# Low parts of queries and keys on GpSimd, a later place in ScalarE's queue for a gated tile's split, and a ninth tile for the first pairs' outputs

## The chip, the cores and the metric

The kernel runs on one core of a Trainium2 chip. The metric is the device time of one execution in microseconds (us), as the median of several timed runs. The engines are named as in the profile: PE is TensorE, DVE is VectorE, ACT is ScalarE, POOL is GpSimd, SP is SyncE, which issues all the transfers (DMAs) here.

## What is computed

Three stages follow each other, all in float32 as far as the reference goes:

```python
scores = q @ k.T / sqrt(64) - log(448)          # 4 batches x 12 heads, 448 x 64
x = sigmoid(scores) @ v                          # back to 1792 tokens x 768
xn = x / sqrt(mean(x * x) + 1e-6) * rms_g
g = xn @ w_gate                                  # 768 -> 1536
h = g * sigmoid(g) * (xn @ w_val)
x2 = h @ w_out                                   # 1536 -> 768
out = ((x2 @ w1) * (x2 @ w2) @ w3) @ w_out2      # 768 -> 1024 -> 1024 -> 768
```

The weights and q, k, v arrive as 64-bit floats.

## The kernel before

**Precision.** TensorE multiplies a rounded form of float32 (`F32R`). An operand that has to be exact is split into two such tiles: a high part (a copy that rounds, by ACT or POOL) and a low part (operand minus high part). `mm3` (L294) then makes three matmuls per block: low weights by high data, high weights by low data, high by high (L296, L297, L298). `split2` (L310) splits an activation: ACT copies at L312 (or POOL at L314), DVE subtracts at L315. `split_weight` (L124) splits a weight: copy on ACT (L126) or POOL (L128), subtraction on POOL (L129). Weights that arrive as 64-bit floats are first turned into float32 by five DVE operations, `to_float` (L106, L107, L108, L116, L119).

**Order.** A scheduler orders each engine's instructions when the program is built, so the written order is a priority and not the order on the engine. Every engine then runs its own queue strictly in order.

**Stages.** A *pair* is two heads, 24 in all. The first 12 pairs (two batches) run at the start: `visit` computes the scores of a pair (`scores`, four column blocks c; L390), ACT takes their sigmoid (L407, L419, L421), `attend` multiplies them with the values (L430, L434), and `take_out` copies the result to a tile `xr` (L457), squares it on ACT (L465, L468) and lets POOL add the squares (L469). These tiles stay on the chip until the normalised x of their batch is made from them (`load_x`, L499, on DVE). There are eight such tiles (`A1`, `xr=8`).

Beside and after these pairs, `w3o_group` multiplies w3 by w_out2 beforehand (L339 to L341; ACT copies the result out, L343). Then `a_group` (L608) makes a gated tile `h` for each of 12 row blocks m and two batches b: a group with `which == 0` gives g, ACT takes its sigmoid (L621) and DVE multiplies (L622); the group with `which == 1` gives the value product, DVE multiplies again (L626) and `split2` splits the tile into `hm` (L312 on ACT, L315 on DVE). In the first six row blocks the groups of b = 1 borrow the PSUM tiles of the attention scores (`psa`).

The other 12 pairs run beside the second half of these groups and beside the first five `b_group` (x2 = h @ w_out; ACT copies out at L635). For these pairs q and k are split too: `load_qk` loads them (L374), and `split_qk` makes the high part on ACT (L381) and the low part on DVE (L382), 128 x 960 elements in one instruction. Their scores (L394) need both parts. The tail of the program (from about 530 us) is further products in a seven-product block scheme (`winograd`).

Of the kernel before, what the change touches and what calls it, by code (L numbers as in the profile page):

```python
# [11 lines left out]
AF = mybir.ActivationFunctionType  # L12
ALU = mybir.AluOpType
# [30 lines left out]
def fused_kernel(ctx: ExitStack, tc: tile.TileContext, qkv, wg, wv, wo, w1, w2, w3, wo2, gam, out):  # L44
    nc = tc.nc

    def pool(name, side=None, space=None):
        kw = {}
        if side:
            kw["side"] = side  # L50
        if space is not None:
            kw["space"] = space
        return tc.alloc_tile_pool(name=name, bufs=1, **kw)
# [29 lines left out]
    def scratch(name):  # L83
        return scr.tile([P, S], F32, tag="s", bufs=6, name=name)
# [215 lines left out]
    def accumulate(tiles, xts, ps=None):  # L300
        ps = psm()[:, :S] if ps is None else ps
        n = len(xts)
        j = 0
        for t, kt in tiles:
            for kw in range(kt):
                mm3(ps, t, kw, xts[j], j == 0, j == n - 1)
                j += 1
        return ps

    def split2(dst, src, scalar=True):  # L310
        if scalar:
            nc.scalar.activation(dst[:, 0, :], src, AF.Copy)  # L312
        else:
            nc.gpsimd.tensor_copy(out=dst[:, 0, :], in_=src)  # L314
        nc.vector.tensor_tensor(out=dst[:, 1, :], in0=src, in1=dst[:, 0, :], op=ALU.subtract)  # L315
# [30 lines left out]

    A1 = dict(raw=3, a=5, al=2, xr=8, wd=2)
    A2 = dict(raw=1, v=2, qk=1, a=3, al=2, xr=2)  # L350
    att = {"bufs": A1, "pool": pool("att1", "left")}

    def at(shape, dtype, tag):
        return att["pool"].tile(shape, dtype, tag=tag, bufs=att["bufs"][tag], name=tag)

    raw, probs, av, acc = {}, {}, {}, {}
# [19 lines left out]
    def split_qk(p):  # L376

        if p < NP:
            t, v, r = at([P, 2, V0], F32R, "qk"), at([P, RAWW - V0], F32, "v"), qk_raw.pop()
            nc.sync.dma_start(out=v, in_=qkv[p // HP, p % HP][:, V0:])  # L380
            nc.scalar.activation(t[:, 0, :], r, AF.Copy)  # L381
            nc.vector.tensor_tensor(out=t[:, 1, :], in0=r, in1=t[:, 0, :], op=ALU.subtract)  # L382
            raw[p] = (t, v)

    def score(ps, p, ds, k):
# [50 lines left out]
    def visit(p, n):  # L436


        if n[0] < p < n[1]:
            scores(p, 3)  # L440
        if p > n[0]:
            attend(p - 1)
            take_out(p - 1)
            if p + n[2] < n[1] and p < NA:
                load_pair(p + n[2])
        if p < n[1]:
            for c in range(3 if p > n[0] else 4):
                scores(p, c)
            if p >= NA:
                split_qk(p + 1)  # L450
                load_qk(p + 2)
# [54 lines left out]
    def split_x(b, k):  # L506

        if k < KD:
            ready.append(load_x(b, k))
        if k:  # L510
            t = acts["x", b, k - 1] = x_tile("x", b)
            split2(t, ready.pop(0), b == 1)
# [7 lines left out]
    def right_blocks(k, b11, b12, b21, b22):  # L520

        tt = nc.vector.tensor_tensor

        def put(j, bl, src):
            t = acts["w", j, k] = right_tile(f"w{j}", bl)
            split2(t, src)

        t1 = scratch("t1")
        put(0, 0, b11)
        tt(out=t1, in0=b12, in1=b11, op=ALU.subtract)  # L530
        put(5, 1, t1)
        put(2, 0, b21)
        tt(out=t1, in0=b22, in1=t1, op=ALU.subtract)
        put(1, 2, t1)
        tt(out=b12, in0=b22, in1=b12, op=ALU.subtract)
        put(3, 2, b12)
        tt(out=b21, in0=b21, in1=t1, op=ALU.subtract)
        put(4, 2, b21)
        put(6, 1, b22)
# [47 lines left out]
    def a_winograd(m):  # L587
        def done(b, g, v):
            s = scratch("s")
            nc.scalar.activation(s, g, AF.Sigmoid)  # L590
            nc.vector.tensor_tensor(out=s, in0=g, in1=s, op=ALU.mult)
            nc.vector.tensor_tensor(out=s, in0=s, in1=v, op=ALU.mult)
            acts["h", b, m] = t = h_tile("hm", m)
            split2(t, s)

        winograd(i_a2, m, done)
# [10 lines left out]
    def h_tile(name, m):  # L607
        return pools[f"h{int(m >= KF1 // 2)}"].tile([P, 2, S], F32R, tag="h", bufs=KF1, name=name)  # L608
# [3 lines left out]
    def a_group(m, b, which):  # L612
        t = W.get(i_a[m][which])
        ps = None
        if b and m < KF1 // 2:

            ps = ps_sc.tile([P, 2, 512], F32, tag="sc", bufs=2, name="psa")[:, 0, :S]
        ps = accumulate([(t, 6)], [acts["x", b, k] for k in range(KD)], ps)
        if which == 0:
            s = scratch("s")  # L620
            nc.scalar.activation(s, ps, AF.Sigmoid)  # L621
            nc.vector.tensor_tensor(out=s, in0=ps, in1=s, op=ALU.mult)  # L622
            half[m, b] = s
        else:
            s = half.pop((m, b))
            nc.vector.tensor_tensor(out=s, in0=ps, in1=s, op=ALU.mult)  # L626
            t = h_tile("hm", m)
            split2(t, s)
            acts["h", b, m] = t

    def b_group(g, m, b):
        t = [(W.get(i), 6) for i in (i_b2 if g else i_b)[m]]
        ps = accumulate(t, [acts["h", b, k] for k in range(KF1)])
        y = scratch("yf")
        nc.scalar.activation(y, ps, AF.Copy)  # L635
        d = yd[g, b, m] = dram.tile([P, S], F32, name=f"y{g}{b}{m}")
        nc.sync.dma_start(out=d, in_=y)
# [8 lines left out]
    def a_units():  # L646
        for m in range(KF1):
            for b in range(2):
                for which in range(2):
                    yield 3.4, (lambda m=m, b=b, w=which: a_group(m, b, w)), i_a[m][which]  # L650

    def b_units(g):
        for m in range(KD):
            for b in range(2):
                yield 6.8, (lambda m=m, b=b: b_group(g, m, b)), (i_b2 if g else i_b)[m][1]
# [62 lines left out]
    a = list(a_units())  # L718
# [7 lines left out]
    pools["h1"] = pool("h1", "right")  # L726
    load_qk(NA)
    split_qk(NA)
    load_qk(NA + 1)
    visits = []  # L730
# [3 lines left out]
    for j, u in enumerate(beside):  # L734
        spent += run(u, int(j >= half_a and j % 2 == 1))

        if 1 <= j <= 3:
            for c in ((0, 1), (2,), (3,))[j - 1]:
                scores(NA, c)
            if j == 3:  # L740
                split_qk(NA + 1)
                load_qk(NA + 2)
            visits = list(range(NA + 1, NP + 1))
        while j > 3 and visits and NP + 1 - NA - len(visits) < (NP + 1 - NA) * (spent - 8.0) / (total - 8.0):
            visit(visits[0], (NA, NP, 1))
            if visits.pop(0) == NA + HP:
                rms_norm(2)
# [93 lines left out]
```

## Time and profile before

| | |
|---|---|
| median of three timed runs | 1113.01 us (1110.99 to 1113.87) |
| the profiled execution, its own time | 1109.31 us |
| its span, first to last instruction | 1107.4 us |
| mean granted TensorE clock | 0.989 |
| busy, share of span: PE, DVE, POOL, ACT | 97%, 73%, 43%, 36% |

A busy PE is not a PE at its peak: a matmul of 448 columns is shown as about 0.37 us long, while the next begins 0.2 us after it. So PE's losses are read from the waits (which engine it waited for, how long), from the windows (how much of a stretch, at which granted clock), and from the chain of waits (the work that ended last, followed back from the end). A group of instructions is named by its line, its engine and its tiles, as in `L382 DVE TENSOR_TENSOR qk<-raw,qk`.

### The profile page before, as it was taken

What the parts mean: (1) busy time and instruction counts of PE and PEld (TensorE: products, weight loads), DVE (VectorE), ACT (ScalarE), POOL (GpSimd) and SP (SyncE); (2) the same over time, 40 slices, a digit from 0 to 9 for tenths busy, and PEclk for the clock granted to TensorE, in tenths of its full rate; (3) what the DMA queues carried; (4) which work ended last, traced back from release to release, by engine and by line L of the source; (5) the groups of instructions that cost most, each with busy time, mean ns of one, the idle gap of its engine ahead of it and who ended that gap; (6) DMA issues with size and microseconds to landing.
All of it is one profiled execution on the core that took longest, in us unless ns stands there. A gap on an engine that the chain in (4) does not pass through costs nothing.

```text
span 1107.4 us, 14309 instructions
## 1 busy us (share of the span) xinstructions
PE 1075.0 (97%) x5236; PEld 907.6 (82%) x5236; DVE 813.4 (73%) x1066; ACT 398.6 (36%) x719; POOL 472.3 (43%) x382
## 2 busy tenths in 40 slices
PE   9989999997899998999999999999999999999998
PEld 4337899995677775799889988999999999999997
DVE  5988998898456688579899989776777645777500
ACT  5764201111444442414544443133443344333221
POOL 2655443443034323333566664222656424656320
PEclk9989999998899999999999999999999999999999
DMA  6733454567445477664212212766221243210131
GB/s 252 253 138 129 148 175 142 166 199 255 138 140 167 130 238 242 200 205 145 82 58 70 73 59 85 235 251 222 84 77 65 67 156 116 91 57 30 48 99 50
DMA packets 62710, 153.25 MB, mean 138 GB/s; under 512 B 6064, under 2 KB 32816, under 8 KB 62640
## 3 DMA queue, kind: packets, MB, share of 16 engines
q1 hardware_dynamic: 62640, 152.33, 40.9%
q8 instruction: 42, 0.69, 0.3%
q14 instruction: 28, 0.23, 0.1%
HBM read 114.95 MB, written 37.36 MB: 138 GB/s over the span
## 4 chain that ended last, share of the span: by engine, by line
PE 64%; DVE 7%; DMA 2%; ACT 2%; issue 1%; POOL 1%; SPq 0%; DVEq 0%; ACTq 0%; POOLq 0%
PE psm L296 10%; PE w L296 10%; PE psm L297 10%; PE w L297 10%; PE psm L298 10%; PE w L298 10%; PE av L434 2%; DVE wf L108 1%; PE psm L394 1%; DVE wf L116 1%; DMA wd<-in_wo 1%; DVE mag L107 1%; PE sc L394 1%; POOL ws L129 1%; DVE wf L119 1%
## 5 line engine op out<-in xcount | busy, mean ns | idle before, releaser
L296 PE MATMUL w<-w,ws 128*128 128x448 f32 x588 | 216.8, 369 | 1.6 <-DVE c L574 1.3
L297 PE MATMUL w<-w,ws 128*128 128x448 f32 x588 | 216.2, 368 | 0.0
L298 PE MATMUL w<-w,ws 128*128 128x448 f32 x588 | 215.6, 367 | 0.0
L129 POOL TENSOR_TENSOR ws<-wf,ws 128x768 fp32r<-128x768 f32 (+1 forms) x88 | 149.5, 1699 | 136.1 <-ACT ws L126 131.9
L129 POOL TENSOR_TENSOR ws<-wd,ws 128x384 fp32r<-128x384 f32 x112 | 126.3, 1142 | 94.9 <-ACT ws L126 86.9
L129 POOL TENSOR_TENSOR ws<-s,ws 128x384 fp32r<-128x384 f32 x84 | 97.2, 1162 | 79.0 <-ACT ws L126 77.3
L128 POOL CAST ws<-wf 128x768 fp32r<-128x768 f32 (+1 forms) x52 | 46.8, 900 | 185.4 <-PE psm L298 90.9
L296 PEld LDWEIGHTS w<-w,ws 128*128 128x128 f32 x588 | 110.3, 188 | 14.6 <-issue 3.7
L298 PEld LDWEIGHTS w<-w,ws 128*128 128x128 f32 x588 | 110.4, 188 | 10.9
L297 PEld LDWEIGHTS w<-w,ws 128*128 128x128 f32 x588 | 110.4, 188 | 10.4
L296 PE MATMUL psm<-hm,ws 128*128 128x448 f32 x288 | 106.7, 370 | 0.0
L297 PE MATMUL psm<-hm,ws 128*128 128x448 f32 x288 | 105.8, 367 | 0.0
L298 PE MATMUL psm<-hm,ws 128*128 128x448 f32 x288 | 105.2, 365 | 0.0
L312 ACT ACTIVATE hm<-s 128x448 fp32r<-128x448 f32 x48 | 27.8, 579 | 213.8 <-DVE s L626 156.8
L108 DVE TENSOR_SCALAR wf<-mag 128x768 uint32<-128x768 uint32 (+1 forms) x76 | 64.4, 847 | 39.4 <-POOL ws L129 35.7
L116 DVE SCALAR_TENSOR_TENSOR wf<-wd,wf 128x768 uint32<-128x768 uint32 (+1 forms) x76 | 86.3, 1136 | 2.3
L296 PE MATMUL psm<-x,ws 128*128 128x448 f32 x216 | 82.0, 380 | 6.1 <-ACT w3ot L343 3.4
L119 DVE SCALAR_TENSOR_TENSOR wf<-wd,wf 128x768 uint32<-128x768 uint32 (+1 forms) x76 | 80.2, 1055 | 1.4
L297 PE MATMUL psm<-x,ws 128*128 128x448 f32 x216 | 80.1, 371 | 0.0
L298 PE MATMUL psm<-x,ws 128*128 128x448 f32 x216 | 79.9, 370 | 0.0
L106 DVE TENSOR_SCALAR mag<-wd 128x768 uint32<-128x768 uint32 (+1 forms) x76 | 49.3, 649 | 32.1 <-DMA wd<-in_wo 21.1
L126 ACT ACTIVATE ws<-wd 128x384 fp32r<-128x384 f32 x112 | 54.6, 514 | 50.2 <-PE w L298 36.3
(131 smaller groups left out, 2159.1 us busy)
## 6 DMA issues: line engine op xcount, KB each, us to landing
wd<-in_wo SPq DMA_DIRECT2D x20, 768.0 KB, 5.7
wd<-in_w SPq DMA_DIRECT2D x16, 768.0 KB, 5.0
wd<-w SPq DMA_DIRECT2D x32, 384.0 KB, 3.4
wd<-in_wg SPq DMA_DIRECT2D x12, 768.0 KB, 4.6
wd<-in_wv SPq DMA_DIRECT2D x12, 768.0 KB, 4.8
wd<-in_w SPq DMA_DIRECT2D x16, 512.0 KB, 4.5
raw<-in_qkv SPq DMA_DIRECT2D x11, 736.0 KB, 4.2
w<-wf SPq DMA_DIRECT2D x16, 384.0 KB, 2.6
```

Of the source, the lines that this page charges most:

```text
L106: nc.vector.tensor_scalar(out=mag.bitcast(U32), in0=hi, scalar1=0x7FFFFFFF, scalar2=None, op0=ALU.bitwise_and)
L108: nc.vector.tensor_scalar(out=u, in0=mag.bitcast(U32), scalar1=3, scalar2=0x3FFFFFFF, op0=ALU.logical_shift_left, op1=ALU.bitwise_and,)
L116: nc.vector.scalar_tensor_tensor(out=u, in0=hi, scalar=0xC0000000, in1=u, op0=ALU.bitwise_and, op1=ALU.bitwise_or)
L119: nc.vector.scalar_tensor_tensor(out=u, in0=lo, scalar=29, in1=u, op0=ALU.logical_shift_right, op1=ALU.bitwise_or)
L126: nc.scalar.activation(t[:, 0, :w], f[:, :w], AF.Copy)
L128: nc.gpsimd.tensor_copy(out=t[:, 0, :w], in_=f[:, :w])
L129: nc.gpsimd.tensor_tensor(out=t[:, 1, :w], in0=f[:, :w], in1=t[:, 0, :w], op=ALU.subtract)
L296: nc.tensor.matmul(ps, wl, xt[:, 0, :], start=first, stop=False)
L297: nc.tensor.matmul(ps, wh, xt[:, 1, :], start=False, stop=False)
L298: nc.tensor.matmul(ps, wh, xt[:, 0, :], start=False, stop=last)
L312: nc.scalar.activation(dst[:, 0, :], src, AF.Copy)
L394: nc.tensor.matmul(o, r[0][d, kj, k], r[0][d, qj, Q0 : Q0 + S], start=(i == 0), stop=(i == 2))
```

## The change

Three edits, with no change to what is computed:

1. The low part of queries and keys (12 instructions, one for each of the second 12 pairs) is subtracted by POOL instead of DVE.
2. The split of a gated tile is not traced with the tile. The tile is put on a list, and `gated()` splits the oldest one right after the *next* sigmoid of an `a_group` is traced, or at the start of a `b_group`. The ACT half of it is pinned: `keep_in_program_order` makes the scheduler leave it in the written order on ACT.
3. There are nine `xr` tiles for the first 12 pairs instead of eight.

```diff
-    def split2(dst, src, scalar=True):
+    def split2(dst, src, scalar=True, pin=False):
         if scalar:
-            nc.scalar.activation(dst[:, 0, :], src, AF.Copy)
+            i = nc.scalar.activation(dst[:, 0, :], src, AF.Copy)
+            if pin:
+                tc.keep_in_program_order(i)
...
-    A1 = dict(raw=3, a=5, al=2, xr=8, wd=2)
+    A1 = dict(raw=3, a=5, al=2, xr=9, wd=2)
...
             nc.scalar.activation(t[:, 0, :], r, AF.Copy)
-            nc.vector.tensor_tensor(out=t[:, 1, :], in0=r, in1=t[:, 0, :], op=ALU.subtract)
+            nc.gpsimd.tensor_tensor(out=t[:, 1, :], in0=r, in1=t[:, 0, :], op=ALU.subtract)
             raw[p] = (t, v)
...
             nc.scalar.activation(s, ps, AF.Sigmoid)
+            gated()
             nc.vector.tensor_tensor(out=s, in0=ps, in1=s, op=ALU.mult)
...
             t = h_tile("hm", m)
-            split2(t, s)
+            unsplit.append((t, s))
             acts["h", b, m] = t
 
+    unsplit = []
+
+    def gated():
+
+        if unsplit:
+            split2(*unsplit.pop(0), pin=True)
+
     def b_group(g, m, b):
+        gated()
```

The new lines shift the numbers by two from L318 on: L381 and L382 of before are L383 and L384 in the change, L621 is L623, L343 is L345, L421 is L423, L419 is L421, L407 is L409, L469 is L471; L312 and its neighbours keep theirs (the DVE half of the split is L317 in the change).

**First place: ACT, where the second 12 pairs begin** (about 241 us in the trace of before). `s<-psm` and `s<-psa` are sigmoids of gated groups, `hm<-s` the split, `qk<-raw` the high part of a pair's queries and keys, `a` and `al` the attention's sigmoids. Before:

```order
L343 ACTIVATE w3ot<-psm 128x384 x2
L621 ACTIVATE s<-psm 128x448
L381 ACTIVATE qk<-raw 128x960
L312 ACTIVATE hm<-s 128x448
L621 ACTIVATE s<-psa 128x448
L312 ACTIVATE hm<-s 128x448
L621 ACTIVATE s<-psm 128x448
L312 ACTIVATE hm<-s 128x448
L421 ACTIVATE a<-sc,bias_s 128x896 x2
L621 ACTIVATE s<-psm 128x448
```

With the change:

```order
L345 ACTIVATE w3ot<-psm 128x384 x2
L383 ACTIVATE qk<-raw 128x960
L623 ACTIVATE s<-psm 128x448
L312 ACTIVATE hm<-s 128x448
L623 ACTIVATE s<-psa 128x448
L312 ACTIVATE hm<-s 128x448
L623 ACTIVATE s<-psm 128x448
L312 ACTIVATE hm<-s 128x448
L423 ACTIVATE a<-sc,bias_s 128x896 x2
L623 ACTIVATE s<-psm 128x448
```

The first sigmoid now stands behind `qk<-raw` and not ahead of it. The rows after it read alike, but each `hm<-s` is now the split of the tile before: the third one of before belongs to the tile of row block 6, b = 0, and waits for that tile's last product (L626); with the change that tile's split comes after the last row shown.

**Second place: POOL, late in the same stretch.** `ws` is the split of a weight, `acc` the sum of squares. Before:

```order
L469 TENSOR_TENSOR acc<-acc,sq 128x448 x2
L128 CAST ws<-wf 128x768
L129 TENSOR_TENSOR ws<-wf,ws 128x768
L128 CAST ws<-wf 128x768
L129 TENSOR_TENSOR ws<-wf,ws 128x768
L469 TENSOR_TENSOR acc<-acc,sq 128x448
```

With the change:

```order
L471 TENSOR_TENSOR acc<-acc,sq 128x448
L384 TENSOR_TENSOR qk<-raw,qk 128x960
L128 CAST ws<-wf 128x768
L129 TENSOR_TENSOR ws<-wf,ws 128x768
L128 CAST ws<-wf 128x768
L129 TENSOR_TENSOR ws<-wf,ws 128x768
L471 TENSOR_TENSOR acc<-acc,sq 128x448
```

A subtraction of queries and keys follows the sum of squares of a pair, ahead of the next weights.

**Third place: DVE, about 430 us in the trace of before,** where it converts weights. Before:

```order
L119 SCALAR_TENSOR_TENSOR wf<-wd,wf 128x768
L106 TENSOR_SCALAR mag<-wd 128x768
L107 TENSOR_SCALAR mag<-mag 128x768
L382 TENSOR_TENSOR qk<-raw,qk 128x960
L108 TENSOR_SCALAR wf<-mag 128x768
L116 SCALAR_TENSOR_TENSOR wf<-wd,wf 128x768
```

With the change:

```order
L119 SCALAR_TENSOR_TENSOR wf<-wd,wf 128x768
L106 TENSOR_SCALAR mag<-wd 128x768
L107 TENSOR_SCALAR mag<-mag 128x768
L108 TENSOR_SCALAR wf<-mag 128x768
L116 SCALAR_TENSOR_TENSOR wf<-wd,wf 128x768
```

The subtraction no longer stands behind two operations of a weight's conversion. PE's own order is the same but for one swap of two neighbours.

## Rows read from the trace of the kernel before

**Rows 1.** The page's part 4: the chain that ended last, by engine.

```profile
PE 64%; DVE 7%; DMA 2%; ACT 2%; issue 1%; POOL 1%; SPq 0%; DVEq 0%; ACTq 0%; POOLq 0%
```

**Rows 2.** Waits of PE, 0 to 500 us: us in total, times, longest.

```profile
PE psm L394 <- DVE qk L382: 6.8, 3, 4.5
PE av L430 <- ACT xr L457: 3.8, 1, 3.8
PE psm L394 <- DVE s L626: 3.6, 1, 3.6
PE psm L296 <- ACT w3ot L343: 3.4, 4, 1.5
PE sc L394 <- issue: 2.9, 1, 2.9
PE psm L296 <- DVE s L622: 2.6, 2, 2.3
```

**Rows 3.** Windows: length; PE, PEld, DVE, ACT, POOL busy (instructions); clock; DMA share, GB/s.

```profile
75.00:80.00 5.00, 5.00 (x14) 1.24 (x12) 3.37 (x8) 3.42 (x6) 1.91 (x2) 0.51 0.00 0
280.00:290.00 10.00, 8.97 (x36) 8.20 (x37) 5.02 (x9) 3.36 (x6) 2.67 (x2) 0.77 0.35 118
250.00:475.00 225.00, 207.05 (x1040) 158.45 (x1040) 157.02 (x186) 85.62 (x131) 65.80 (x46) 0.96 0.57 189
```

**Rows 4.** Timeline of ACT, 60 to 126 us: start, length, instruction [idle before, until].

```profile
73.84 0.54 ACT L457 ACTIVATE xr<-av 128x448 f32<-128x448 f32 x1 [8.03 <-DVE xs L499]
...
104.19 0.58 ACT L480 ACTIVATE t<-v 128x448 f32<-128x448 f32 x1
...
119.26 0.58 ACT L312 ACTIVATE x<-xs 128x448 fp32r<-128x448 f32 x1 [12.40 <-DVE xs L499]
119.74 0.47 ACT L343 ACTIVATE w3ot<-psm 128x384 f32<-128x384 f32 x1
```

**Rows 5.** Timeline of DVE, 74 to 120 us.

```profile
77.15 0.62 DVE L315 TENSOR_TENSOR x<-xs,x 128x448 fp32r<-128x448 f32 x1 [1.53 <-POOL x L314]
...
109.08 2.94 DVE L481 RECIPROCAL r<-t 128x448 f32<-128x448 f32 x1
```

**Rows 6.** Timeline of ACT, 240 to 295 us.

```profile
242.35 0.55 ACT L621 ACTIVATE s<-psm 128x448 f32<-128x448 f32 x1
253.09 1.01 ACT L381 ACTIVATE qk<-raw 128x960 fp32r<-128x960 f32 x1 [10.19 <-DMA raw<-in_qkv]
...
277.51 0.58 ACT L312 ACTIVATE hm<-s 128x448 fp32r<-128x448 f32 x1 [9.47 <-DVE s L626]
278.00 1.89 ACT L421 ACTIVATE a<-sc,bias_s 128x896 f32<-128x896 f32 x2
279.77 0.54 ACT L621 ACTIVATE s<-psm 128x448 f32<-128x448 f32 x1
```

**Rows 7.** Timeline of DVE, 254 to 265 us and at 435 us.

```profile
256.52 0.62 DVE L622 TENSOR_TENSOR s<-psm,s 128x448 f32<-128x448 f32 x1
...
434.96 2.04 DVE L107 TENSOR_SCALAR mag<-mag 128x768 f32<-128x768 f32 x1
436.92 1.15 DVE L382 TENSOR_TENSOR qk<-raw,qk 128x960 fp32r<-128x960 f32 x1
437.99 0.55 DVE L108 TENSOR_SCALAR wf<-mag 128x768 uint32<-128x768 uint32 x1
```

**Rows 8.** The chain of waits in order of time, 438 to 460 us.

```profile
438.12 1.36 PE psm L394 x3
...
445.77 0.41 PE psm L296
...
453.30 0.60 PE psm L394 x3
...
459.07 0.41 PE psm L296
```

**Rows 9.** Timeline of POOL, 428 to 468 us.

```profile
434.59 1.99 POOL L129 TENSOR_TENSOR ws<-wf,ws 128x768 fp32r<-128x768 f32 x1
...
445.04 1.14 POOL L469 TENSOR_TENSOR acc<-acc,sq 128x448 f32<-128x448 f32 x1 [8.46 <-ACT sq L468]
...
463.91 1.84 POOL L129 TENSOR_TENSOR ws<-wf,ws 128x768 fp32r<-128x768 f32 x1
```

## The prediction, made before the change was run

> **What bounds the kernel now.** First the chain that ended last: PE holds 64% of it, DVE 7%, every other engine 2% or less [rows 1]. So time is won only where PE waits. The waits of PE come next: up to 500 us it waited for DVE's low part of queries and keys (L382) for 6.8 us in three waits, the longest 4.5; for ACT's copy of a pair's output (L457) 3.8 us, once; for ACT's copies of w3 products (L343) 3.4 us in four; for DVE's two products of a gated tile (L626, L622) 3.6 and 2.6 us; and 2.9 us once ahead of a pair's scores, where no releaser is shown [rows 2]. The reader is to see that each edit names a line of this list. Last come the windows: PE also loses time after a wait, because the granted clock is lower then, 0.51 in the five microseconds behind the wait for L457, 0.77 around 285 us [rows 3]. All of the rest of the program is left as it is.
>
> **The change part by part.** A positive number is a gain.
>
> *A, the ninth output tile.* The ninth pair's copy (L457) idled 8.03 us until DVE had read the first of eight tiles (L499) [rows 4]. With nine it need not wait, so PE's 3.8 us go, and so does the low clock behind it: 5 us at 0.51 cost about 2.5. That would be 6.3 us, if PE stayed the bound. It doesn't. About 45 us later ACT idled 12.40 us for DVE's L499 of the second batch, and the L343 that PE waits for stands behind that instruction on ACT's queue [rows 4]. DVE in turn was late by its own queue: the root that its reciprocal L481 needs was there at 104.8 (104.19 + 0.58) [rows 4], and DVE came to it at 109.08 [rows 5]. PE arriving six microseconds earlier finds the same DVE. What DVE itself gains is about 1 us, of the 1.53 that it idled for a POOL copy queued behind a sum of squares that waits for the late L457 [rows 5]. Against this, PE's idle time moves to just before 119.7, becomes some 6 us long, and the low clock then falls on work that counts: about 2 us by the window at 0.51, of which over 1 is covered by a second wait for L343 there [rows 2, 3]. I take **+0.5**. Bounds: +6.3 (all of it comes through) and -2 (only the clock's loss does).
>
> *D, the split later, first half of the gated groups.* L343 no longer stands behind the split of the tile just finished. Of the 3.4 us in four waits the longest, 1.5, belongs to A's place and so does one more; I take **+0.8** of the remaining 1.9, bounds 0 and 1.9 [rows 2].
>
> *B, the start of the second 12 pairs, 250 to 300 us.* ACT stood in the split L312 for 9.47 us, waiting for L626, while the scores' sigmoid (L421) and the next gated sigmoid (L621) stood behind it [rows 6]. With the change both are ahead of it. L621 can then run well before the L626 that ends the wait, so L622 follows L626 directly, and of PE's 2.3 us for L622 [rows 2] I count 1.8 as won, plus 0.5 of low clock behind it (0.77 in that window) [rows 3]. But one row stands worse: the first sigmoid is now behind L381, which idled 10.19 us for the load of queries and keys [rows 6]. It moves from 242.35 to about 253.6, and the split behind it to about 254.5. DVE came to the L622 concerned at 256.52 [rows 7], so the sigmoid itself is just in time. POOL, however, now has the first L382 ahead of a weight's split, and DVE's two-input work beside it is held for its length. That puts L622 back by 2 to 4 us and PE with it, though PE's 2.9 us ahead of the scores [rows 2], further down the same path, absorb most of that. I charge 0.8. Sum of B: 1.8 + 0.5 - 0.8 = **+1.5**. Bounds: -3.5 (nothing is absorbed) and +6.5 (no delay, and half of the 3.6, 2.6 and 2.9 us of waits with some clock goes).
>
> *C, L382 on POOL.* The price of one on POOL isn't in the trace. POOL's subtractions are: 448 elements 1.14 us, 768 elements 1.84 [rows 9], so 2.19 ns for each further element, and 960 cost 1.84 + 192 x 2.19 ns = 2.26 us, an estimate; DVE's takes 1.15 [rows 7]. Twelve are 27.1 us on POOL for 13.8 taken from DVE. POOL has room: 65.8 us busy of 225 [rows 3]. Is it in time? Between two visits of a pair PE works 7.5 us on other products (445.77 to 453.30) [rows 8]; ACT's high part ends about 3 us into that, so 2.26 and one held instruction of up to 1 us still fit. The queue decides. At 436.92 the low part came late because DVE had it behind L107, which took 2.04 us [rows 7] beside POOL's L129 [rows 9]. On POOL it stands behind a sum of squares and ahead of that L129. So the 4.5 us go, and the clock's share with them: from L394 to the next long product the visit took 445.77 - 438.12 = 7.65 us, the following one 459.07 - 453.30 = 5.77 [rows 8], a difference of 1.9. The two shorter waits, 2.3 us together [rows 2], are of the same kind. All: 6.8 + 1.9 = 8.7; I take **+8.0**, leaving 0.7 for the longer instruction. Bounds 3 and 8.7.
>
> On DVE, the L108 and L107 that POOL meets are held: L107 took 2.04 us beside L129's 1.99, while L108, with no POOL instruction beside it, took 0.55 [rows 7, 9]. Twelve holds of up to 2.26 us are more than the 13.8 us removed. I cost that at nothing, since DVE was idle for 225 - 157 = 68 us of the stretch [rows 3]; if that cover were gone, it is the last rival below. The Trainium skill (SBUF — State Buffer, Who interferes with whom) says that the pair of ports that the two engines share is locked whole, and that the later one blocks fully; the L107 row agrees.
>
> Sum: 0.5 + 0.8 + 1.5 + 8.0 = **10.8 us**. The profiled execution took 1109.31 us (its span 1107.4 plus 1.9 around it), so 1098.5. The median of the runs lies 3.7 above the profiled one: **1102.2 us**.
>
> **The rivals.**
>
> *Both fronts open.* A comes through whole and B reaches 5: 6.3 + 0.8 + 5 + 8.0 = 20, so 1093. For it: PE's waits in both places are real. Against: DVE's queue at 109 [rows 5].
>
> *The head costs.* The sigmoid behind the load, and POOL's first L382, set PE back by B's lower bound: 0.5 + 0.8 - 3.5 + 8.0 = 5.8, so 1107.2. For it: the 10.19 us [rows 6] now hold a sigmoid and a place on POOL.
>
> *The waits change their names.* PE, free of L382, waits for the next late thing, a product L626 or a converted weight, and C leaves 1 instead of 8: a gain of 0 to 3.3, about 1111. For it: DVE at 434 was itself waiting, and L107 stays [rows 7].
>
> *The port, slower than before.* POOL's 27.1 us hold DVE wherever DVE works beside them. If DVE were the bound over the stretch, 27.1 - 13.8 = 13.3 us are added, less A, B, C and D: 13.3 - 10.8 = +2.5, and with low clock behind the new waits (1.9 each [rows 8], one or two) about 5: 1118. It decides only once DVE's 68 us of idle time [rows 3] lie elsewhere than the holds. Against it: PE isn't waiting for weights in rows 2 at all. The Trainium skill (GPSIMD Engine Reference, Engine selection) speaks against this edit: an elementwise operation on two inputs belongs on VectorE, GpSimd being about twice as slow. The trace's estimate, 2.26 against 1.15, agrees; the rule counts the instruction, and not whose queue is late.
>
> **How the numbers follow.** Chances: the forecast, a gain of 6.5 to 14, 0.46; both fronts open 0.13; the head costs 0.18; the waits change their names 0.15; the port 0.08. About 0.3%, 3.3 us, is what a measurement of this kernel can tell from no change. Faster by more than that: 0.46 + 0.13 + 0.18 = 0.77; within it 0.15; slower 0.08. The range runs from 1094 to 1111: it leaves out the port (0.08), about half of the renamed waits (0.07) and the far end of both fronts (0.05).
>
> **What would show it.** Right: the waits of PE hold no L382 over 1 us; the visit that took 7.65 us takes about 5.8; POOL's subtraction takes 2.2 to 2.5 us; L457 no longer idles for L499, and a PE wait of 4 us or more for L343 appears shortly before 120 us, with a low clock behind it; the sigmoid L621 near 253 us starts right behind the high part. Wrong: that wait is missing and PE is six microseconds earlier at 130 (both fronts); the first product after 257 us waits over 3 us for L622 and the loss is still there at 300 (the head); L626 or L106 take L382's place in PE's waits near 434 (renamed); or PE waits for `ws` from POOL between 300 and 475 (the port).

## The result, and the profile after

The changed kernel took 1099.38 us (median of 4 runs, 1097.01 to 1102.59) beside 1112.0 us for the kernel before (4 runs, 1108.15 to 1113.87): a ratio of 0.9893, interval 0.9855 to 0.9931. A second measurement (below, e8) gave 1101.87 beside 1109.25: 0.9928, 0.9905 to 0.9952. The profiled execution took 1099.9 us, its span 1098.0; before they were 1109.31 and 1107.4, so 9.4 us less.

The page of the kernel after, parts 1 and 4. The second line answers to [rows 1].

```profile
PE 1070.4 (97%) x5236; PEld 908.5 (83%) x5236; DVE 818.7 (75%) x1054; ACT 400.2 (36%) x719; POOL 504.6 (46%) x394
```

```profile
PE 62%; DVE 4%; POOL 1%; ACT 1%; issue 1%; DMA 1%; SPq 0%; ACTq 0%; POOLq 0%; DVEq 0%
```

DVE's share of the chain fell from 7% to 4%. The waits of PE from 0 to 500 us of the kernel after (us in total, times, longest) answer to [rows 2]; the lines of the code have moved by two or three (L457 is now L459, L343 L345, L382 L384, L394 L396, L622 L625, L626 L629):

```profile
PE psm L296 <- ACT w3ot L345: 7.9, 1, 7.9
PE psm L396 <- DVE s L629: 3.4, 2, 1.8
PE sc L396 <- DVE s L629: 3.1, 1, 3.1
...
PE psm L296 <- DVE s L625: 0.9, 1, 0.9
PE psm L396 <- POOL qk L384: 0.7, 1, 0.7
```

The reader is to see three things. The 3.8 us for a pair's output copy are gone. The 6.8 us for the low part of queries and keys have become 0.7, for POOL. And the largest wait of all is new: 7.9 us at once for a copy of a w3 product.

Both kernels issue the same 5236 matmuls in the same order, but for one swap of neighbours at 291 us. So the k-th matmul can be found in both traces, and the difference of its two starts says how far ahead the changed kernel is there. Worked out so (us, before less after):

| place (start before) | what it is | ahead |
|---|---|---|
| 79.27 | behind the old wait for L457 | +6.2 |
| 120.36 | first gated product | -1.2 |
| 128.99 | third gated group (L296 into `psa`) | -2.5 |
| 245.75 | ahead of the second pairs | -0.6 |
| 285.23 | behind their first scores | +7.4 |
| 395.70 | steady part | +6.0 |
| 410.49 | behind a new wait at 397 | +3.9 |
| 444.19 | behind the visit that took 7.65 us | +10.2 |
| 1100.24 | the end | +9.3 |

**The first stall moved, and grew.** The timelines of ACT and of DVE in the kernel after, 94 to 126 us, answer to [rows 4, 5] (start, length, instruction, in brackets idle time before and its end):

```profile
99.06 0.58 ACT L482 ACTIVATE t<-v 128x448 f32<-128x448 f32 x1
...
120.47 0.58 ACT L312 ACTIVATE x<-xs 128x448 fp32r<-128x448 f32 x1 [18.76 <-DVE xs L501]
120.95 0.47 ACT L345 ACTIVATE w3ot<-psm 128x384 f32<-128x384 f32 x1
```

```profile
102.09 0.94 DVE L108 TENSOR_SCALAR wf<-mag 128x768 uint32<-128x768 uint32 x1 [1.19 <-POOL ws L129]
...
107.94 2.49 DVE L116 SCALAR_TENSOR_TENSOR wf<-wd,wf 128x768 uint32<-128x768 uint32 x1
110.35 2.94 DVE L483 RECIPROCAL r<-t 128x448 f32<-128x448 f32 x1
```

The root of the second norm is there at 99.64 (99.06 + 0.58), 5 us sooner than before. DVE comes to its reciprocal at 110.35, 1.3 us later than before, because seven instructions that decode weights are ahead of it on its queue from 102.09. So ACT's x waits until 120.47, and the copy that PE needs stands right behind it.

**The start of the second pairs opened.** ACT, 250 to 275 us, after; [rows 6] is the same place before:

```profile
252.18 1.01 ACT L383 ACTIVATE qk<-raw 128x960 fp32r<-128x960 f32 x1 [12.38 <-DMA raw<-in_qkv]
253.09 0.53 ACT L623 ACTIVATE s<-psm 128x448 f32<-128x448 f32 x1
...
266.19 0.58 ACT L312 ACTIVATE hm<-s 128x448 fp32r<-128x448 f32 x1 [6.10 <-DVE s L629]
266.68 1.89 ACT L423 ACTIVATE a<-sc,bias_s 128x896 f32<-128x896 f32 x2
272.58 0.54 ACT L623 ACTIVATE s<-psm 128x448 f32<-128x448 f32 x1 [4.01 <-issue]
```

The sigmoid of the first scores ran at 278.00 [rows 6]; now it runs at 266.68, and the next gated sigmoid at 272.58 and not at 279.77.

**The visit is short, but something comes late ahead of it.** PE in the kernel after, from 429 us, answers to [rows 8]:

```profile
429.57 0.78 PE L396 MATMUL psm<-qk 128*128 128x448 f32 x3
...
435.46 0.48 PE L296 MATMUL psm<-hm,ws 128*128 128x448 f32 x1
```

From L396 to the next long product it takes 5.89 us instead of 7.65, with no wait ahead. But DVE at 384 to 399 us shows what took some of the gain:

```profile
392.37 0.56 DVE L106 TENSOR_SCALAR mag<-wd 128x768 uint32<-128x768 uint32 x1 [4.39 <-DMA wd<-in_wo]
...
396.96 1.49 DVE L106 TENSOR_SCALAR mag<-wd 128x768 uint32<-128x768 uint32 x1
398.38 0.61 DVE L629 TENSOR_TENSOR s<-psm,s 128x448 f32<-128x448 f32 x1
```

DVE stood 4.39 us for weights from DMA, then had their decode ahead of the gated products. The second L106 took 1.49 us instead of 0.56 beside a sum of squares on POOL, and PE waited for L629:

```profile
396.90 1.13 POOL L471 TENSOR_TENSOR acc<-acc,sq 128x448 f32<-128x448 f32 x1 [6.80 <-ACT sq L470]
```

Windows of the kernel after, with the granted clock (columns as in [rows 3], which has the row of 225 us for before):

```profile
113.00:121.00 8.00, 0.67 (x4) 0.35 (x2) 8.00 (x13) 0.53 (x2) 2.94 (x2) 0.74 0.44 139
121.00:126.00 5.00, 4.43 (x12) 4.00 (x13) 5.00 (x8) 2.10 (x6) 2.42 (x2) 0.50 0.61 182
250.00:475.00 225.00, 215.30 (x1092) 167.28 (x1091) 159.08 (x178) 87.88 (x135) 99.52 (x61) 0.98 0.59 196
401.00:406.00 5.00, 5.00 (x21) 4.50 (x20) 3.91 (x5) 1.45 (x3) 2.85 (x2) 0.75 0.97 347
```

Behind the 7.9 us of idle time PE runs at 0.50, the lower of its two levels (1.2 GHz), on the first gated products. Fifteen of them, from the second on, took 5.3 us instead of 3.0. After the wait at 397 the clock is 0.75. The row of 225 us is not the same work as before's: it holds 1092 matmuls where that one held 1040.

### The profile page after: what moved, and what is told of

Its sections match the earlier page's. It is cut to its first block, busy times and chain, and to the rows that moved or that the text cites. A ratio compares the mean times of both kernels' runs of the same rounds, so it can differ in the third digit from the quotient of the medians.

```text
span 1098.0 us, 14309 instructions
## 1 busy us (share of the span) xinstructions
PE 1070.4 (97%) x5236; PEld 908.5 (83%) x5236; DVE 818.7 (75%) x1054; ACT 400.2 (36%) x719; POOL 504.6 (46%) x394
## 4 chain that ended last, share of the span: by engine, by line
PE 62%; DVE 4%; POOL 1%; ACT 1%; issue 1%; DMA 1%; SPq 0%; ACTq 0%; POOLq 0%; DVEq 0%
PE psm L296 10%; PE psm L297 10%; PE psm L298 10%; PE w L296 9%; PE w L297 9%; PE w L298 9%; PE av L436 2%; POOL ws L129 1%; PE psm L396 1%; DVE s L594 1%; DMA wd<-in_wo 1%; PE sc L396 1%; PE av L432 0%; DVE wd L163 0%; DVE s L161 0%
## 5 line engine op out<-in xcount | busy, mean ns | idle before, releaser
L296 PE MATMUL w<-w,ws 128*128 128x448 f32 x588 | 216.7, 369 | 2.9 <-DVE c L576 1.7
L129 POOL TENSOR_TENSOR ws<-wf,ws 128x768 fp32r<-128x768 f32 (+1 forms) x88 | 153.8, 1748 | 135.9 <-ACT ws L126 131.7
L296 PEld LDWEIGHTS w<-w,ws 128*128 128x128 f32 x588 | 110.3, 188 | 16.1 <-issue 5.3
L297 PEld LDWEIGHTS w<-w,ws 128*128 128x128 f32 x588 | 110.4, 188 | 10.2
L296 PE MATMUL psm<-hm,ws 128*128 128x448 f32 x288 | 106.7, 370 | 0.0
L116 DVE SCALAR_TENSOR_TENSOR wf<-wd,wf 128x768 uint32<-128x768 uint32 (+1 forms) x76 | 94.0, 1237 | 2.5
L108 DVE TENSOR_SCALAR wf<-mag 128x768 uint32<-128x768 uint32 (+1 forms) x76 | 72.0, 947 | 30.2 <-POOL ws L129 25.8
L296 PE MATMUL psm<-x,ws 128*128 128x448 f32 x216 | 82.7, 383 | 8.9 <-ACT w3ot L345 7.9
L106 DVE TENSOR_SCALAR mag<-wd 128x768 uint32<-128x768 uint32 (+1 forms) x76 | 56.2, 739 | 34.4 <-DMA wd<-in_wo 23.7
L297 PE MATMUL psm<-x,ws 128*128 128x448 f32 x216 | 81.3, 376 | 0.0
L298 PE MATMUL psm<-x,ws 128*128 128x448 f32 x216 | 81.0, 375 | 0.0
L119 DVE SCALAR_TENSOR_TENSOR wf<-wd,wf 128x768 uint32<-128x768 uint32 (+1 forms) x76 | 77.2, 1016 | 1.5
L296 PE MATMUL psm<-ab,ws 128*128 128x448 f32 x192 | 70.7, 368 | 0.0
```

The lines of the kernel that those rows point to most:

```text
L106: nc.vector.tensor_scalar(out=mag.bitcast(U32), in0=hi, scalar1=0x7FFFFFFF, scalar2=None, op0=ALU.bitwise_and)
L108: nc.vector.tensor_scalar(out=u, in0=mag.bitcast(U32), scalar1=3, scalar2=0x3FFFFFFF, op0=ALU.logical_shift_left, op1=ALU.bitwise_and,)
L116: nc.vector.scalar_tensor_tensor(out=u, in0=hi, scalar=0xC0000000, in1=u, op0=ALU.bitwise_and, op1=ALU.bitwise_or)
L119: nc.vector.scalar_tensor_tensor(out=u, in0=lo, scalar=29, in1=u, op0=ALU.logical_shift_right, op1=ALU.bitwise_or)
L129: nc.gpsimd.tensor_tensor(out=t[:, 1, :w], in0=f[:, :w], in1=t[:, 0, :w], op=ALU.subtract)
L296: nc.tensor.matmul(ps, wl, xt[:, 0, :], start=first, stop=False)
```

## The experiments

Each kernel ran 6 to 12 times beside the kernel before on the same chip; the median of before was 1108.88 us for e1 to e4 (29 runs), 1109.25 for e5 to e8 (22), 1109.38 for e12 and e13 (11). Single runs of one kernel lie up to 4 to 6 us from their median, so medians tell sizes and the profiles tell places. "Stage" times below are differences of starts of the same matmuls.

**e1: the ninth tile alone.** The kernel before with

```diff
-    A1 = dict(raw=3, a=5, al=2, xr=8, wd=2)
+    A1 = dict(raw=3, a=5, al=2, xr=9, wd=2)
```

> The kernel before with the ninth output tile alone. Theory (DVE's queue holds the gate): PE comes to the w3 products about 6 us earlier than before, then waits 7 to 8 us for the copy of a w3 product, and its first gated product starts at 121 to 122 us instead of 120.4; nothing else moves; time between 0 and 3 us longer than before. Rival (the stall at 70 us was paid in full): first gated product at 114 to 116 us, time 4 to 6 us shorter.

Measured: 1110.32 us, ratio 1.0012 (0.9995 to 1.0029). Its waits of PE:

```profile
PE psm L296 <- ACT w3ot L343: 7.9, 1, 7.9
PE psm L394 <- DVE qk L382: 6.9, 3, 4.5
```

The tile alone makes the new wait, to the tenth of a microsecond, and wins nothing: the third gated group starts 2.7 us later than before, and the time is 1.4 us longer. The theory held, and the rival (all 6.3 come through) fell.

**e2: the later split alone.** The changed kernel with eight tiles, and the low part on DVE:

```diff
-    A1 = dict(raw=3, a=5, al=2, xr=9, wd=2)
+    A1 = dict(raw=3, a=5, al=2, xr=8, wd=2)
-            nc.gpsimd.tensor_tensor(out=t[:, 1, :], in0=r, in1=t[:, 0, :], op=ALU.subtract)
+            nc.vector.tensor_tensor(out=t[:, 1, :], in0=r, in1=t[:, 0, :], op=ALU.subtract)
```

> The kernel before with the later split alone. Theory (most of the gain up to 300 us is ACT's queue): the first scores of the second pairs come 0 to 3 us earlier, PE's fourth sum over the tokens (484.7 us before) 8 to 11 us earlier, with PE's waits for the low part of queries and keys on DVE still 4 us or more in sum; time 7 to 10 us shorter. Rival (DVE relieved of the low parts made that gain): fourth sum 0 to 4 us earlier, time 0 to 4 us shorter.

Measured: 1103.89 us, ratio 0.9956 (0.9937 to 0.9976), 5.0 us shorter; its profiled execution was 7.8 shorter. The fourth sum over the tokens comes 7.8 us earlier. The mechanism is the theory's, but the timed gain lies between the two expectations (7 to 10, and the rival's 0 to 4). From the matmul that starts at 245.75 before to the one at 297.48 it needs 45.25 us where before needs 51.73, so 6.5 us come from the start of the second pairs. Another 1.3 us come between 128.99 and 245.75. At the visit that took 7.65 us before, it still has the old wait, the 3.5 us in this line:

```profile
PE psm L396 <- DVE qk L384: 5.2, 2, 3.5
```

**e3: the low part on POOL alone.** The kernel before with

```diff
-            nc.vector.tensor_tensor(out=t[:, 1, :], in0=r, in1=t[:, 0, :], op=ALU.subtract)
+            nc.gpsimd.tensor_tensor(out=t[:, 1, :], in0=r, in1=t[:, 0, :], op=ALU.subtract)
```

> The kernel before with the low parts on POOL alone. Theory: PE's waits for the low part fall from 6.8 us to under 1.5, and the visit at 438 us takes 5.8 instead of 7.7, but other waits take part of it: fourth sum over the tokens 2 to 6 us earlier, time 2 to 6 us shorter. Rival (as forecast, C's 8.0 us stand alone): 7 to 9 us shorter. Second rival (the port): no shorter, or longer.

Measured: 1104.15 us, ratio 0.9957 (0.9938 to 0.9976), 4.7 us shorter. Its waits of PE:

```profile
PE psm L296 <- DVE s L626: 2.0, 1, 2.0
PE psm L394 <- POOL qk L382: 1.9, 2, 1.0
```

The wait of 4.5 us is gone, and between 431.83 and 444.19 it needs 5.99 us against 12.36: 6.4 us won in that one place. But between 403.59 and 410.49, where before needs 6.90 us, it needs 9.26: the L626 of the first row is at that place. Here the moved subtraction itself holds DVE, whose L106 took 1.60 us instead of 0.56:

```profile
397.38 2.26 POOL L382 TENSOR_TENSOR qk<-raw,qk 128x960 fp32r<-128x960 f32 x1 [7.89 <-ACT qk L381]
```

```profile
398.46 1.60 DVE L106 TENSOR_SCALAR mag<-wd 128x768 uint32<-128x768 uint32 x1 [1.44 <-DMA wd<-in_wo]
```

The theory held in the time and in the places, but PE's waits for the low part stayed at 1.9 us where it had under 1.5. The profile also tells how far one profile can be trusted: up to 250 us PE, DVE, ACT and POOL run the same instructions in the same order as before, and still this one is 3.4 us late at 245.75.

**e6: the change without the POOL edit**, that is the ninth tile and the later split.

```diff
-            nc.gpsimd.tensor_tensor(out=t[:, 1, :], in0=r, in1=t[:, 0, :], op=ALU.subtract)
+            nc.vector.tensor_tensor(out=t[:, 1, :], in0=r, in1=t[:, 0, :], op=ALU.subtract)
```

> The change with the low parts back on DVE (later split and ninth tile together). Theory (edits add up, the POOL move is worth 3 to 5 us, the ninth tile nothing): time 3 to 6 us longer than the change, PE's waits for the low part 4 us or more in sum again. Rival (the later split alone made the gain): within 1.5 us of the change.

Measured: 1107.34 us, ratio 0.9975 (0.9957 to 0.9992); the whole change beside it (e8) is 5.5 us shorter, as the theory has it. So the POOL edit is worth 4.7 on top of nothing and 5.5 on top of the others. Between 403.59 and 410.49 it needs 6.97 us, and e2, also without POOL's subtractions, 7.60: without them the wait at 397 is absent or short.

**e4: the change with eight tiles.**

```diff
-    A1 = dict(raw=3, a=5, al=2, xr=9, wd=2)
+    A1 = dict(raw=3, a=5, al=2, xr=8, wd=2)
```

> The change with eight output tiles, so without its third edit. Theory: the wait of 7.9 us at 120 is gone, PE's stall at 70 is back, the first gated product is at 119 to 121 us, and the rest follows: 1 to 3 us shorter than the change (about 14 us shorter than before). Rival (the ninth tile helps): 2 to 6 us longer than the change.

Measured: 1098.39 us, ratio 0.9906 (0.9881 to 0.9931), between the two measurements of the whole change (0.9893, 0.9928). The rival, that the tile pays once the other edits are made, fell. In the profile the places are the theory's: the first gated product starts at 120.31, and the third gated group at 128.94, as before, against 131.46. That the tile costs 1 to 3 us isn't shown by the times. By the ratios eight tiles are 2.4 us faster here than nine in e8, 2.1 in e2 than in e6 and 1.3 in the kernel before than in e1, each within the noise; against the first measurement of the change eight tiles are 1.4 slower.

**e7: the first low part on DVE, the other eleven on POOL.**

```diff
-            nc.gpsimd.tensor_tensor(out=t[:, 1, :], in0=r, in1=t[:, 0, :], op=ALU.subtract)
+            e = nc.vector if p == NA else nc.gpsimd
+            e.tensor_tensor(out=t[:, 1, :], in0=r, in1=t[:, 0, :], op=ALU.subtract)
```

> The change with only the first pair's low part back on DVE. Theory (POOL's first subtraction holds DVE's two-input operation for 2 us at 254 us, and PE's first wait for L625 follows from it): the operation that took 2.90 us takes about 1, PE's first score of the second pairs is 0 to 2 us earlier; time 0 to 2 us shorter than the change. Rival (the hold is absorbed further down): no difference at the first sum after the pairs' start, within 0.5 us.

Measured: 1100.34 us, ratio 0.9924 (0.99 to 0.9947), against e8's 0.9928. The matmul that started at 297.48 before starts at 290.80 here and at 290.79 in e8. DVE's L119 takes 0.96 us here, as the theory has it, but PE's first score comes no earlier. What the first POOL subtraction sets back is absorbed on the way, as the rival has it.

**e8: the change again**, unedited, beside e5 to e7.

> The change again, as it is, beside the three others on one chip. Both theories: 9 to 13 us shorter than the kernel before; it is the yardstick for the other three.

Measured: 1101.87 us, ratio 0.9928 (0.9905 to 0.9952), 7.4 us shorter, which is less than the 9 to 13 expected. Its profile has the same 7.9 us wait and loses 1.1 us at the place where the first profile loses 3.8 (8.04 us for 6.90). There L106 started before POOL's sum of squares and took 0.55 us; in the first profile it started behind it (396.96 and 396.90) and took 1.49:

```profile
397.66 0.55 DVE L106 TENSOR_SCALAR mag<-wd 128x768 uint32<-128x768 uint32 x1
```

```profile
397.79 1.42 POOL L471 TENSOR_TENSOR acc<-acc,sq 128x448 f32<-128x448 f32 x1 [6.81 <-ACT sq L470]
```

DVE, ACT and POOL run the same instructions in the same order in both profiles. So the size of the wait at 397 hangs on a tenth of a microsecond. The other profiles agree: where L106 is ahead of the sum (e12, e13) 1.1 and 1.0 us are lost at this place, where it is behind (e5, e7) 4.3 and 3.9, and in e4, where the sum holds L119 just before it, 4.7.

**e5: the high parts of the second batch's x on POOL**, in the changed kernel, to free ACT's queue ahead of the w3 copies.

```diff
-            split2(t, ready.pop(0), b == 1)
+            split2(t, ready.pop(0), False)
```

> The change, with the high parts of the second batch's x copied by POOL and not by ACT, so that the copies of w3 products no longer stand on ACT behind x tiles that wait for DVE. Theory (that place on ACT's queue is why the ninth tile brought nothing): PE's wait of 7.9 us for the copy of a w3 product falls under 2, the first gated product starts at 113 to 116 us instead of 121.6, PE then waits for x tiles or weights from DVE, and the third group, the first that needs the second batch, starts 2 to 5 us earlier than in the change; time 2 to 5 us shorter than the change. Rival (DVE is the gate whatever ACT does): the idle time moves to the third group and nothing is left, within 1 us of the change.

Measured: 1103.61 us, ratio 0.9945 (0.9925 to 0.9966). ACT, 108 to 134 us:

```profile
124.25 0.87 ACT L345 ACTIVATE w3ot<-psm 128x384 f32<-128x384 f32 x2 [17.82 <-DVE x L317]
```

The first gated product starts at 114.05 instead of 121.57, then PE waits 6.9 us for the next copy, and the third group starts at 131.30 against 131.46. The copy no longer waits on ACT's queue: it waits for a scratch tile, which DVE's x chain gives back with L317. So the wait has a second gate behind the first, and the rival (the idle time moves, nothing is left) held; the time is 1.7 us longer than e8's, within the noise.

**e12: two tiles of their own for the w3 copies**, in the changed kernel.

```diff
-        o = scratch("w3ot")
+        o = at([P, NH], F32, "w3t") if kt < W3_FIRST else scratch("w3ot")
-    A1 = dict(raw=3, a=5, al=2, xr=9, wd=2)
+    A1 = dict(raw=3, a=5, al=2, xr=9, wd=2, w3t=2)
```

> The change with two tiles of their own (128x384) for the copies that L345 makes while the attention of the first pairs runs, in place of the six shared scratch tiles that the x chain of VectorE and ScalarE holds. Theory (the stall before the first gated product is made by two things, the scratch tiles and ScalarE's in-order queue, in which the copy stands behind three high parts of x that wait for VectorE): the tiles alone change little, since the queue still holds the copy; the wait of PE for L345 stays above 4 us and the third group starts within 1.5 us of the change's 131.46 us. Rival (the tiles alone are the gate): the wait falls below 2 us, the first gated product starts at about 114 us and the third group 3 to 7 us earlier, and the time is 3 to 6 us shorter than that of the change.

Measured: 1099.12 us, ratio 0.99 (0.9877 to 0.9924); the wait:

```profile
PE psm L296 <- ACT w3t L345: 3.9, 1, 3.9
```

It halved, and the third group starts at 129.68. Both expectations were missed: the theory had the wait above 4 us and the third group within 1.5 us of 131.46, the rival had the wait below 2 and the group 3 to 7 us earlier. The tiles and the queue are a gate each.

**e13: these tiles and e5's edit together.**

> The same tiles, and the high parts of the last batch's x by POOL in place of ScalarE, so that both suspected gates are away: ScalarE's queue has nothing ahead of the copies, and the tiles are free. Theory: the wait of PE for L345 falls below 2 us in all, the first gated product starts at 113 to 115 us, and the products of the third group then wait for x itself, which VectorE is making until about 130 us; so the group starts 0 to 4 us before 131.46 us, and the time is 0 to 4 us shorter than the change's. Rival (x of the last batch is what sets the third group, whatever holds the copies): the idle time moves to the third group whole, which starts within 1 us of 131.46 us or later, and the time is that of the change or up to 3 us longer.

Measured: 1101.67 us, ratio 0.9929 (0.9905 to 0.9952). No wait for L345 is left. Its waits of PE, and its windows from 121 us:

```profile
PE psa L297 <- DVE x L317: 3.0, 5, 1.1
```

```profile
121.00:126.00 5.00, 3.36 (x12) 1.64 (x10) 4.55 (x8) 1.83 (x2) 2.79 (x5) 1.00 0.00 0
126.00:131.00 5.00, 2.67 (x6) 1.40 (x6) 4.55 (x6) 0.00 (x0) 3.71 (x4) 0.56 0.48 137
```

The third group starts at 121.53, ten microseconds early, which neither expected, and then goes at the pace at which DVE hands out x. At the matmul that started at 160.18 before, it is at 161.80 and the change at 162.49. So the rival is right in what counts: with both gates away x itself sets this place, which DVE makes behind its late reciprocal, and nothing is left of the six microseconds.

No version beat the change by more than the intervals; e12 has the shortest span, 1096.7. An edit that puts the reciprocal ahead of the decode on DVE's queue wasn't tried, so that the reciprocal's place is the last gate is read from the traces and not shown by a run. Nor were the two parts of the later split, its place and its pin, run apart.

## Why the prediction was right

**The total.** 1098.5 us was forecast for the profiled execution, and it was 1099.9; 1102.2 for the median, measured 1099.38 and 1101.87. The forecast case (a gain of 6.5 to 14) is the one that came: 9.4 us by the profiles, 12.6 and 7.4 by the medians. That the sum of 10.8 fits so well is partly luck. B was 2 to 7 us too small, A 2 to 3 and C about 3 too large, and they cancelled. The time forecast for the median leaned on three runs of the kernel before, 3.7 us above its profiled execution; the later runs of that kernel have medians of 1108.88 to 1109.38, level with it.

The signs that were to show the forecast right all came in the first profile: 0.7 us of waits for the low part, the visit in 5.89 us, POOL's subtraction at 2.27, the 7.9 us wait with a clock of 0.50 behind it, and the sigmoid at 253.09, right behind the high part. In e8 the wait for the low part is 1.5 us, above the 1 us that was named.

**A, the ninth tile: +0.5 forecast.** The step was that PE, six microseconds early, finds the same DVE, and that the stall moves to just before 120 us with low clock behind it. e1 shows that whole. But at the third group the term has the other sign: the kernels with nine tiles that differ in nothing else up to there are 1.8 to 2.7 us late (e1 2.7, the changed kernel 2.5, e8 1.9, e6 1.8), around the lower bound of -2. Two things were under-counted. The stall is 7.9 us and not some 6, since the reciprocal came 1.3 us later than before and not one earlier. And the low clock cost 2.3 us, without the second wait for the copy that was to cover over 1 of it. By time e1 took 1.4 us longer than before, with an interval that holds no change.

**D, the split later in the first half: +0.8.** e2 gains 1.3 us between 128.99 and 245.75. The changed kernel gains 1.9 there, but e1, without the split, gains 1.1, so D itself is 0.7 to 1.3, as forecast.

**B, the start of the second pairs: +1.5, the term that was furthest off.** e2 shows 6.5 us in this stage, the whole change 8.1 and e8 6.7; in e6 and e4, where one wait for L629 was longer (3.6 us), 3.8 and 3.5. Some of it isn't the split's: e1 and e3, which come to 245.75 1.5 and 3.4 us late, make up 2.7 and 2.1 there.

I had counted the 2.3 us wait for L622 and a little clock, and charged 0.8 for POOL's first low part. What came in its place is the scores' sigmoid, eleven microseconds earlier, which pulls the first pair forward. The split is its cause: in every kernel with the later split this sigmoid starts 20.0 to 21.4 us behind the matmul of 245.75, in the kernel before, e1 and e3 29.2 to 32.2 us. The waits of PE from 245 to 298 us add up to 11.5 us before and 6.3 after: the 3.6 us for L626 became 1.6, and the 2.6 for L622 became 0.9, while the 2.9 us ahead of the scores stayed under another name (L629, 3.1). The other 2.9 us go with the clock, 0.87 before and 0.97 after in this window. I had kept L626's part and most of the clock's for the upper bound, +6.5, which the first profile passes. The charge of 0.8 was for nothing (e7). The held instruction itself came as forecast: DVE's L119 took 2.90 us beside POOL's first L384 of 2.53. The Trainium skill (SBUF — State Buffer, Who interferes with whom) has it that issue order decides who blocks; these rows agree, POOL having started at 253.26 and DVE's L119 at 253.71.

```profile
253.26 2.53 POOL L384 TENSOR_TENSOR qk<-raw,qk 128x960 fp32r<-128x960 f32 x1 [5.03 <-DMA v<-in_qkv]
```

```profile
253.71 2.90 DVE L119 SCALAR_TENSOR_TENSOR wf<-wd,wf 128x768 uint32<-128x768 uint32 x1
```

**C, L382 on POOL: +8.0, over-sized by about 3.** e3 gives 4.7, e8 against e6 5.5, and e4 against e2 5.5 as well. The price of the instruction was right: 2.26 us estimated, this row of the line's view of the changed kernel (least, median, most, ns):

```profile
L384 POOL TENSOR_TENSOR qk<-raw,qk x12: 2247/2271/2740, 253.3 to 440.3; 128x960 fp32r<-128x960 f32 x12
```

The wait of 4.5 us and the 1.9 us of low clock in the visit came too, 6.3 us together in the changed kernel and 6.4 in e3. What failed is the step "I cost that at nothing, since DVE was idle for 225 - 157 = 68 us of the stretch". That idle time is an average, and it doesn't lie at 397 us. There DVE has waited for `wd`, has the decode and the gated products in a row behind it, and one held instruction is passed on to PE, with low clock after: 2.4 us in e3, where the moved subtraction itself is the holder. In the seven profiles that have the POOL edit beside the later split 1.0 to 4.7 us are lost there, in the four without the POOL edit 0 to 0.7.

How the POOL edit does it in the changed kernel isn't shown. The holder there is the sum of squares, which the kernel before has too, and DVE's wait for `wd`, 1.37 us before and 4.39 in the change, is 3.59 in e2 as well. What differs from e2 and e6 is DVE's own order: in the change a weight's L116 stands ahead of the gated product L625, in these two behind it.

How much was held is seen in DVE's busy time over the whole program, from part 1 of the pages of the kernel before, e3 and e6:

```profile
PE 1075.0 (97%) x5236; PEld 907.6 (82%) x5236; DVE 813.4 (73%) x1066; ACT 398.6 (36%) x719; POOL 472.3 (43%) x382
```

```profile
PE 1074.3 (97%) x5236; PEld 908.8 (82%) x5236; DVE 807.8 (73%) x1054; ACT 398.4 (36%) x719; POOL 504.9 (46%) x394
```

```profile
PE 1073.1 (97%) x5236; PEld 908.4 (82%) x5236; DVE 823.4 (75%) x1066; ACT 399.6 (36%) x719; POOL 473.7 (43%) x382
```

The POOL edit took DVE from 813.4 to 807.8 us alone, and from 823.4 to 818.7 on top of the others: about 5 us less, where twelve subtractions, 15.4 and 13.8 us in all, had gone. So 9 to 10 us, some two thirds, came back as longer instructions. The windows of 225 us (157.02 and 159.08) can't tell this: they don't hold the same work, and the later split alone adds 9 us to DVE (822.2 in e2).

**The rivals.** Both fronts open: one did, the second pairs; the first didn't (e1, e13). The head costs: fell (e7). The waits change their names: the mechanism is real and took 1 to 5 us at 397, not 7. (Its own sum is 0.5 + 0.8 + 1.5 + 1 = 3.8, a little over the 3.3 that it gave as its most.) The port: its holds are in the trace, and it never became the bound. The rule that speaks against two-input work on GpSimd (the Trainium skill, GPSIMD Engine Reference, Engine selection) is right on the instruction, 2.27 us against 1.15, and the move still gained 5 us, since the queue that the instruction left was the late one.

What stays open is the attribution within some 3 us inside a stage: it rests on single profiles, which differ by that much where nothing was edited (e3 ahead of 250 us), and the waits for L629 fall differently from one to the next.

## What to carry to other kernels

A stall is worth removing only if what stands next in line is also ready: before counting it, find the next instruction that another in-order queue delivers late, and see whether anything in the edit moves that. A slower engine can be the better place for an operation when the faster one has it behind other work, but its holds on the neighbour must then be looked for at every place where that neighbour is itself just in time, and not averaged over a stretch. Where a wait sits at the head of a pipeline, the term is the whole chain behind it and not the one wait that names it.

## What the runs showed that was not expected

A split that was moved on ACT pulled the first scores' sigmoid from 278.00 to 266.68 us, and in e2, with that edit alone, the stage was 6.5 us shorter, while the longest single wait of that stage was 3.6 us. Taking away the two gates on one copy, each alone and then both, gave 7.9, 6.9, 3.9 and then 0 us of wait (the change, e5, e12, e13) and no time clear of the noise: behind them stands x itself, and by the traces a reciprocal queued behind seven decode instructions. A tenth of a microsecond in the start of one instruction decided whether 1 or 4 us were lost at another place, in two profiles of the same kernel. And POOL's 960-element subtraction cost what two shorter ones extrapolate to, 2.27 us for 2.26.
